# A list-scheduled attention kernel: tap copies spread in time, later and shared PSUM banks, and a new order of the schedule

## The chip, the cores and the metric

One core of one Trainium2 chip. The metric is the device time of one execution in microseconds (us), median of several. Nearly all executions of a kernel agree within 0.3%; one execution of the kernel before took 926.79 us, is not a fast run and is left out of every comparison. A profile's span is about 2 us shorter than the device time of the same run.

Engines: PE (matmul), PEld (its weight loads), DVE (VectorE), ACT (ScalarE), POOL (GpSimd), SP (issues the DMAs).

## The reference, cut to what matters

Two attentions over the same `x` (2048 tokens, 640 wide, 32 heads of 20), mixed by a gate:

```python
g = sigmoid((x * gate_w).sum(-1, keepdims=True))
a = A_ref(x, A_wqkv, A_wo)   # full softmax attention, 32 heads, 2048 x 2048 scores each
b = B_ref(x, B_wqkv, B_wo)   # sliding window: 8 keys per query, at distances 0, 2, ..., 14
return g * a + (1 - g) * b
```

Attention A needs 32 x 2048 x 2048 exponentials. The kernel cuts them into 2048 *units*: one unit is one head, 128 keys and 512 queries, that is 512 columns on 128 partitions.

## The kernel before

The program is written by a small planner inside the kernel. It places every task by an estimated duration, engine by engine. A main loop lays tile after tile of attention A; everything else ("side work": projections, window attention B, folds into the output) is a set of generators that get a turn when PE has a gap.

```python
score = [ps(1536, "score0"), ps(1536, "score1")]      # 3 PSUM banks each
obank = ps(512, "obank")
sbank = ps(512, "side0")
BANKS = [(sbank, 0), (score[0], 1024), (score[1], 1024)]   # banks that side work may take
```

So the PSUM's eight banks are: two scores of three banks each, one output accumulator, one private side bank. The *third* bank of each score is shared. A tile always has two units; if the third bank is free, a third unit goes into it, and this *third position* is used in one of two ways:

```python
def next_tile():
    free = not bank_used[x] and bank_free[x] <= now + XTOL and not crowded(x)
    n = 3 if free else 2
    while len(us) < n and cur["g"] < NG:
        ...
        if len(us) == 2 and not ride:
            ride = wanted([...])      # DVE makes this exponential by integer shifts (a "ride")
            if ride:
                break
        us.append(g * 64 + lo)        # else ACT takes 1536 columns in one piece
```

If side work holds the third bank, ACT takes 1024 columns. Side work asks for a bank by priority (a lower number goes first). The private bank is open to all; a score's bank is not:

```python
elif req[0] == "bank":
    ...
    if best and not force and (ent[0] > xprio() or any(...)):   # best 1 or 2: a score's bank
        return False

def xprio():     # how low a priority may still take a score's bank
    return XPRIO if bdone[0] >= (sch.avail["pe"] - XT0) / (XT1 - XT0) * BALL else XLATE
```

`XPRIO` is 2.5. `XLATE` (6.6) holds when the window work is behind its pace. The priorities are 5 for folds, 6 for window blocks, 6.5 for their projections, so before the change all three may take a score's bank when window work is late.

Three more pieces of side work: the weights of attention B are spread by POOL (the "tap copies"), in bursts; the window block takes a bank; the fold takes four bank turns.

```python
def gen_bweights():
    for m in (2, 0, 1):
        ...
        for c in range(CN):            # five copies in a row on POOL
            T("pool", 1.6, lambda e, o=o, i=i: e.tensor_copy(o, i), ...)

def gen_fold(qc, hu):                  # waits for window block 2*qc+hu and for A's heads
    for blk in (2 * hu, 2 * hu + 1):
        for hf, (c0, c1) in enumerate(((0, 512), (512, D))):
            b = yield from bank()      # also for the 128 columns left over
            ...
```

`gen_prefold` does the same for the last quarter of the tokens and needs the last window block (`gen_b(7)`); only then can the last output rows be finished.

## Time and profile before

| | before |
|---|---|
| device time, fast runs | 873.97 to 875.44 us, median of the four runs 875.15 with the slow one |
| span of the profile | 872.9 us |
| PE / ACT / DVE / POOL busy | 98% / 95% / 78% / 25% |
| exponentials on ACT (L1410) | 815.6 us in 785 pieces |
| units by ride on DVE (L1400) | 300 of 2048 |

The profile page of the kernel before, part 1 (busy us, share of the span, instructions):

```profile
PE 852.7 (98%) x13106; PEld 308.0 (35%) x13106; DVE 680.7 (78%) x1157; ACT 831.0 (95%) x819; POOL 221.1 (25%) x324
```

PE's 98% is not what it seems: the kernel fills PE's gaps with matmuls whose result nobody reads (L1476), and they count as busy. The Trainium skill, "Perfetto Trace Analysis", Identifying the Most-Contended Engine, says that a busy PE is not a good measure of its nearness to its limit and that for ACT and DVE the busy share is a fair one. PE's share misleads for a further reason, the kernel's own: 1472 filler matmuls, 114 of the 853 us, are in the busy count. ACT is the engine to look at.

The groups view of the kernel before, shapes kept apart (line, engine, operation, out and in, count, busy us, mean ns, idle before, what ended it):

```profile
L1410 ACT ACTIVATE ebuf<-score 128x1024 bf16<-128x1024 f32 x607 | 581.6, 1035 | 16.1 <-PE score L1387 12.6 <-ACT ebuf L1410 0.3
L1410 ACT ACTIVATE ebuf<-score 128x1536 bf16<-128x1536 f32 x178 | 251.1, 1476 | 4.7 <-PE score L1387 4.5
L1400 DVE TENSOR_SCALAR uD<-score 128x512 int16<-128x512 f32 x300 | 201.9, 684 | 59.4 <-PE score L1387 57.2 <-ACT g L671 0.5
L489 PE MATMUL side<-xT,kvw 128*32 128x256 bf16 x1380 | 57.4, 276 | 0.4 <-DVE qkvB L773 0.2
L489 PE MATMUL score<-xT,kvw 128*32 128x256 bf16 x1020 | 41.8, 274 | 0.0
```

The third positions: 178 wide pieces on ACT and 300 rides on DVE, 478 together. The last two lines are B's projections: 1020 of their 2400 matmuls write into a score's bank.

Waits of ACT, and the end of the run (groups in order of time: start, us, what) of the kernel before:

```profile
ACT ebuf L1410 <- PE score L1387: 17.1, 53, 1.6
ACT stage L969 <- PE side L950: 6.7, 1, 6.7
```

```profile
841.89 0.42 DVE L880 SCALAR_TENSOR_TENSOR oB<-side,rB 128x256 bf16<-128x256 f32 x1 [0.28 <-PE side L489]
...
856.74 3.77 ACT L1410 ACTIVATE ebuf<-score 128x1536 bf16<-128x1536 f32 x3 [0.24 <-PE score L1387]
867.19 0.60 ACT L969 ACTIVATE stage<-side 128x512 bf16<-128x512 f32 x1 [6.68 <-PE side L950]
```

The first of these lines is the last task of the last window block: it ends at 842.3 us. The last exponential ends at 860.5 us, the run at 872.9 us: a *tail* of 12.4 us.

### The profile page before, as it was taken

The numbers are of one execution on the slowest core, as the hardware profiler recorded it, in microseconds if no ns is written. First come the engines' busy times: TensorE is split into PE (matmuls) and PEld (weight loads), VectorE is DVE, ScalarE is ACT, GpSimd is POOL, SyncE is SP. The second block draws the span as 40 slices with busy tenths as digits, with TensorE's granted clock in tenths as the row PEclk, the third lists the DMA queues.
The fourth block names the chain that finished last, engine by engine and source line by source line (L and its number), as shares of the span: only waits on it lengthen the run. The fifth ranks groups of instructions, "written<-read, shape, count | busy, mean of one in ns | idle before, by whom it ended". The sixth has DMA issues, their size and how long they took to land.

```text
span 872.9 us, 30620 instructions
## 1 busy us (share of the span) xinstructions
PE 852.7 (98%) x13106; PEld 308.0 (35%) x13106; DVE 680.7 (78%) x1157; ACT 831.0 (95%) x819; POOL 221.1 (25%) x324
## 2 busy tenths in 40 slices
PE   8999999999999999999999999999999999999997
PEld 4333233333333333343333333333333334433233
DVE  6567777698988797779687787798788758889953
ACT  5999999899999999999999999999999999999994
POOL 5032014622332231112232122323104312023310
PEclk9999999999999999999999999999999999999999
DMA  9111212101011010010000110010001000100100
GB/s 296 32 38 42 44 34 51 36 15 30 26 28 24 28 36 16 13 37 21 20 18 14 30 26 19 29 27 16 12 20 34 21 19 30 30 6 9 27 6 32
DMA packets 40891, 28.15 MB, mean 32 GB/s; under 512 B 23732, under 2 KB 39556, under 8 KB 40756
## 3 DMA queue, kind: packets, MB, share of 16 engines
q1 hardware_dynamic: 40756, 26.20, 11.3%
q8 instruction: 104, 1.70, 0.8%
q14 instruction: 31, 0.25, 0.1%
HBM read 11.94 MB, written 2.62 MB: 17 GB/s over the span
## 4 chain that ended last, share of the span: by engine, by line
PE 73%; ACT 17%; DVE 6%; issue 4%; DMA 0%; POOL 0%; SPq 0%; DVEq 0%; ACTq 0%
PE score L1387 23%; PE obank L1455 17%; ACT ebuf L1410 16%; PE side L489 14%; PE score L489 9%; PE obank L1476 3%; PE score L1476 2%; PE side L1476 1%; DVE uD L1400 1%; DVE eD L720 1%; DVE stage L789 1%; DVE qkvB L773 1%; PE side L802 1%; PE score L609 1%; DVE stage L865 0%
## 5 line engine op out<-in xcount | busy, mean ns | idle before, releaser
L1410 ACT ACTIVATE ebuf<-score 128x1024 bf16<-128x1024 f32 (+1 forms) x785 | 815.6, 1135 | 20.8 <-PE score L1387 17.1
L1387 PE MATMUL score<-qT,kT 32*128 32x512 bf16 x2048 | 315.0, 385 | 11.0 <-ACT ebuf L1410 4.9
L1400 DVE TENSOR_SCALAR uD<-score 128x512 int16<-128x512 f32 x300 | 201.9, 684 | 59.4 <-PE score L1387 57.2
L712 POOL TENSOR_SCALAR vS<-vA 128x84 bf16<-128x84 bf16 x225 | 142.8, 638 | 161.4 <-PE obank L1455 151.8
L1387 PEld LDWEIGHTS score<-qT,kT 32*128 32x128 bf16 x2048 | 77.7, 91 | 277.4 <-issue 113.3
L1455 PE MATMUL obank<-ebuf,vA 128*21 128x512 bf16 x1748 | 167.4, 385 | 1.2 <-ACT ebuf L1410 0.9
L720 DVE TENSOR_SCALAR eD<-uD 128x2048 int16<-128x2048 int16 x225 | 154.7, 712 | 7.6 <-PE obank L1455 7.0
L687 POOL TENSOR_TENSOR rcp<-rcp,gA 128x16 f32<-128x16 f32 x31 | 10.5, 337 | 429.1 <-DVE rcp L685 429.1
L1455 PE MATMUL obank<-eD,vS 128*21 128x512 bf16 x900 | 78.3, 379 | 0.0
L1455 PEld LDWEIGHTS obank<-ebuf,vA 128*21 128x21 bf16 x1748 | 41.4, 89 | 85.0 <-issue 70.3
L489 PE MATMUL side<-xT,kvw 128*32 128x256 bf16 (+1 forms) x1540 | 70.5, 287 | 0.4 <-DVE qkvB L773 0.2
L489 PE MATMUL score<-xT,kvw 128*32 128x256 bf16 (+1 forms) x1220 | 60.4, 292 | 0.0
L1476 PE MATMUL obank<-xT,zero 128*32 128x512 bf16 x680 | 55.7, 384 | 0.0
L789 DVE TENSOR_TENSOR stage<-qkvB 128x1280 bf16<-128x1280 bf16 x64 | 53.3, 859 | 0.1
L865 DVE TENSOR_TENSOR stage<-qkvB,repB 128x1280 bf16<-128x1280 bf16 x64 | 53.2, 856 | 0.1
L489 PEld LDWEIGHTS side<-xT,kvw 128*32 128x32 bf16 x1540 | 36.9, 96 | 24.4 <-issue 15.0
L489 PE MATMUL side<-stage,ident 128*32 128x512 bf16 (+1 forms) x672 | 44.9, 352 | 0.0
L1476 PE MATMUL score<-xT,ident 128*32 128x512 bf16 x424 | 36.7, 381 | 0.0
L489 PEld LDWEIGHTS score<-xT,kvw 128*32 128x32 bf16 x1220 | 28.6, 96 | 22.3 <-issue 15.2
L692 POOL TENSOR_TENSOR oN<-oTt,rcp 128x512 bf16<-128x512 f32 x31 | 34.9, 1124 | 2.4
L681 DVE STREAM_TRANSPOSE oTt<-obank 128x512 f32<-128x512 f32 x32 | 22.8, 712 | 15.3 <-PE obank L1455 15.0
L1455 PE MATMUL obank<-uD,vA 128*21 128x512 bf16 x300 | 29.2, 379 | 0.0
(174 smaller groups left out, 686.6 us busy)
## 6 DMA issues: line engine op xcount, KB each, us to landing
repB<-eB SPq DMA_DIRECT2D x128, 32.0 KB
WqP<-in_A_wqkv_dram SPq DMA_DIRECT2D x16, 160.0 KB
stage<-in_B_wqkv_dram SPq DMA_DIRECT2D x1, 2400.0 KB
oTd<-oN SPq DMA_DIRECT2D x108, 20.0 KB
qT<-dst SPq DMA_DIRECT2D x104, 20.0 KB
out_dram<-outsb SPq DMA_DIRECT2D x12, 160.0 KB
kvw<-in_A_wqkv_dram SPq DMA_DIRECT2D x2, 800.0 KB
oTd<-in_A_x_dram SPq DMA_DIRECT2D x2, 640.0 KB
```

Source lines behind the costliest of these rows:

```text
L489: ins = e.matmul(o[j:k, :], l[:, j:k], r, start=(first and i == 0), stop=(last and i == n - 1), skip_group_check=True)
L681: T("dve", dvc(512), lambda e: e.transpose(oTt[:, :], obank[:, :]), reads=["obank"], writes=["oTt"])
L692: T(en, c2, lambda e: e.tensor_tensor(oo, ii, ib, ALU.mult), reads=["rcp", "oTt"], writes=["oN0"])
L712: T("pool", 0.7, lambda e, k=k: e.tensor_scalar(vS[:, d % 2, k - 1, :], _ap(vA, (kb * NQ + q) * 4 * DV, [[1, 4 * DV]]), WEIGHTS[k], None, ...
L720: T("dve", 0.11 + 0.1334 * n, lambda e, k=k, sl=sl: e.tensor_scalar(eD[:, sl % NS, 0:512 * n].bitcast(I16), uD[d % 2][:, 0:512 * n].bitcas ...
L789: TB(dvc(CN * TOK, 2), lambda e, w=w, ks=ks: e.tensor_tensor(prodB(w), qB[:, :, :], ks, ALU.mult), reads=["qB", "kB"], writes=[("prod", w) ...
L865: TB(dvc(CN * TOK, 2), lambda e, w=w, vs=vs, rr=rr: e.tensor_tensor(prodB(w), vs, rr, ALU.mult), reads=["vB", ("repB", w4 % 2)], writes=[( ...
L1387: ins = e.matmul(o, kT[32 * j:32 * j + 32, q, kb * P:(kb + 1) * P], qT[g % NQT][32 * j:32 * j + 32, :], start=True, stop=True)
L1400: t = T("dve", 0.69, lambda e: e.tensor_scalar(uD[d % 2][:, 512 * i:512 * (i + 1)].bitcast(I16), side[x], UOFF, 0.0, op0=ALU.add, op1=ALU. ...
L1410: exps[s] = T("act", actc(512 * n), lambda e: e.activation(ebuf[s % NE][:, 0:512 * n], score[s % 2][:, 0:512 * n], ACTF.Exp, scale=LN2 / S ...
L1455: ins = e.matmul(obank[32 * j:32 * j + DV, :], v, src, start=(kb == 0), stop=(last and k >= len(lst) - 4), skip_group_check=True)
L1476: ins = e.matmul(o[32 * j:32 * j + 32, :], w[:, 32 * j:32 * j + 32] if best else w[:, :], xT[:, 0, 0:512], start=bool(best), stop=bool(bes ...
```

## The change

The intent: take the POOL burst apart, hold PSUM banks for a shorter time and fewer turns, and lay the schedule in an order tuned for that. Nothing of the arithmetic changes. The core of the diff:

```diff
 # tap copies: the next one only when POOL is not behind PE
             for c in range(CN):
+                while sch.avail["pool"] > max(sch.avail["pe"], clock[0]):
+                    yield ("cond",)
 # QK sums: the bank is taken when the operand is nearly ready
+                yield ("pe", 0.0, sch.ready(("qabs", (n - 1) % 2)) - 0.2)
                 b = yield from bank()
 # window logits: likewise
+        yield ("pe", 0.0, sch.ready(*[("prod", w) for w in range(WIN)]) - 0.7)
         b = yield from bank()
 # B projections: nine bank turns a block become eight, two of the three leftovers share one
-        for m in range(3):
-            for f0 in range(0, CN, 2):
+        for grp in (((0, 0), (0, 1)), ((0, 2), (0, 3)), ((1, 0), (1, 1)), ((1, 2), (1, 3)), ((0, 4), (1, 4)),
+                    ((2, 0), (2, 1)), ((2, 2), (2, 3)), ((2, 4),)):
 # fold: the two 128-column remainders share one bank, four turns become three
+        b = yield from bank()
+        for k in range(2):
+            yield from mm_group(b, mms(side[b][:, k * P:(k + 1) * P], 2 * hu + k, 512, D), rd, mmc(P), per=3)
 ...                                      (a BATCH table that batches nothing; other cuts)
 # order
-    DVE_AHEAD = 0.4          +    DVE_AHEAD = 0.56
-    BOOST = 4.5              +    BOOST = 4.1
-    XLATE = 6.6              +    XLATE = 6.3
-    XT0 = 150.0              +    XT0 = 144.0
-    QPRIO, KPRIO = 0.9, 2.0  +    QPRIO, KPRIO = 1.1, 1.2     # two lines in the kernel
-    BT1 = 880.0              +    BT1 = 927.0
-    XTOL = 0.2               +    XTOL = 0.17
-    DLOW = 7.0               +    DLOW = 6.7
-    SLACK = (0.3, 0.7)       +    SLACK = (0.3, 0.68)
-    fold priority 5          +    PF = 6.6                    # window 6 and projections 6.5 stay
```

More of the change, by code (lines that the diff above doesn't have):

```diff
@@ L572, in _build @@
     qkeys = {}
+    BATCH = (0, 1, 2, 3, 4)
     def gen_qd():
@@ L578, in gen_qd @@
         for qc in range(QCN):
+            batch = []
             for f in range(CN):
@@ L601, in gen_qd @@
                   reads=[("dst", i)], writes=[("qabs", n % 2)])
+                batch.append(f)
+                n += 1
+                if BATCH[f] != f:
+                    continue
+                fl = [(ff, (n - 1 - f + ff) % 2) for ff in range(max(0, batch[0] - 1), f + 1)]
+                yield ("pe", 0.0, sch.ready(("qabs", (n - 1) % 2)) - 0.2)
                 b = yield from bank()
-                fl = [(f - 1, (n + 1) % 2)] if f else []
-                fl.append((f, n % 2))
-                yield ("pe", mmc(512) * len(fl), sch.ready(("qabs", n % 2)))
+                yield ("pe", mmc(512) * len(fl), sch.ready(("qabs", (n - 1) % 2)))
                 def fn(e, b=b, fl=fl):
@@ L618, in gen_qd @@
                 release(b, t)
+                pc = [p_ for ff in batch for p_ in pieces[ff] if p_[0] >= 4 or qc > 1]
+                gs = sorted({POS[qc, p_[0] // 4] for p_ in pc})
                 hs = [h for h, o, r, m in pc if r + m == DH]
@@ L630, in gen_qd @@
                   dma=True, nd=len(runs))
-                n += 1
                 for q in range(NQ):
-                    if chunks_of(q)[-1] == f and (q or qc > 1):
+                    if chunks_of(q)[-1] in batch and (q or qc > 1):
                         g = POS[qc, q]
                         qkeys[g] = [("qTd", g % NQT, ff) for ff in chunks_of(q)] + [
-                            ("qTb", g % NQT, ff) for ff in sorted({max(ff for ff in range(CN) for p_ in pieces[ff] if p_[0] == h)
+                            ("qTb", g % NQT, ff) for ff in sorted({BATCH[max(ff for ff in range(CN) for p_ in pieces[ff] if p_[0] == h)]
                                                                    for h in range(4 * q, 4 * q + 4)})]
                         done[("q", g)] = True
+                batch = []
     def gen_v(half):
@@ L753, in gen_bproj @@
                 T("dve", 0.1, lambda e, t_=t_: e.memset(t_[:, :, 0:PADB], 0.0), writes=[key, ("kst", 0), ("kst", 1)])
-        for m in range(3):
+        for grp in (((0, 0), (0, 1)), ((0, 2), (0, 3)), ((1, 0), (1, 1)), ((1, 2), (1, 3)), ((0, 4), (1, 4)),
+                    ((2, 0), (2, 1)), ((2, 2), (2, 3)), ((2, 4),)):
+            m, f0 = grp[0]
             while m == 2 and u > 0 and not done.get(("bp", u - 1)):
                 yield ("cond",)
-            if u > 0 and m > 0:
+            if u > 0 and m > 0 and f0 == 0:
@@ L758, in gen_bproj @@
                 bb, key = ((kB, "kB"), (vB, "vB"))[m - 1]
                 TB(0.15, lambda e, bb=bb: e.tensor_copy(bb[:, :, 0:PADB], bb[:, :, TOK:TOK + PADB]), reads=[key], writes=[key])
-            for f0 in range(0, CN, 2):
-                fs = range(f0, min(CN, f0 + 2))
-                b = yield from bank()
-                for f in fs:
-                    mms = [(side[b][:, (f - f0) * TOK:(f - f0 + 1) * TOK],
-                            kvw[:, (m * CN + c) * D + f * P:(m * CN + c) * D + (f + 1) * P],
-                            xT[:, c, t0:t0 + TOK]) for c in range(CN)]
-                    yield from mm_group(b, mms, [("wBp", m)] + XT(t0 // 512), mmc(TOK), first=True, per=2)
-                yield ("dve",)
-                n = len(fs)
-                tt, off, key = dst[m]
-                o = tt[:, f0:f0 + n, off:off + TOK]
-                i = sap(b, 0, [[TOK, n], [1, TOK]])
+            b = yield from bank()
@@ new lines, in gen_bproj @@
+            for k, (mm_, f) in enumerate(grp):
+                mms = [(side[b][:, k * TOK:(k + 1) * TOK],
+                        kvw[:, (mm_ * CN + c) * D + f * P:(mm_ * CN + c) * D + (f + 1) * P],
+                        xT[:, c, t0:t0 + TOK]) for c in range(CN)]
+                yield from mm_group(b, mms, [("wBp", mm_)] + XT(t0 // 512), mmc(TOK), first=True, per=2)
+            yield ("dve",)
+            parts = [(m, f0, len(grp))] if grp[0][0] == grp[-1][0] else [(mm_, f, 1) for mm_, f in grp]
@@ L773, in gen_bproj @@
+            for k, (mm_, f, n) in enumerate(parts):
+                tt, off, key = dst[mm_]
+                o = tt[:, f:f + n, off:off + TOK]
+                i = sap(b, k * TOK, [[TOK, n], [1, TOK]])
                 t = TB(dvc(n * TOK), lambda e, o=o, i=i: e.tensor_copy(o, i), reads=[("side", b)], writes=[key])
-                release(b, t)
-            if m == 1:
+            release(b, t)
+            if grp == ((0, 4), (1, 4)):
                 done[("bqk", u)] = True
@@ L883, in gen_b @@
         done[("b", u)] = True
-    pre = lambda i: (dst2[:, 0:1024], qabs2[:, :], stage[:, 2048:3072])[i].bitcast(FP32)
+    pre = lambda i: (dst2[:, 0:1024], qabs2[:, 0:1024], stage[:, 2048:3072])[i].bitcast(FP32)
     tail_bank = {}
@@ L982, in gen_fold, with mms @@
             yield ("cond",)
-        for blk in (2 * hu, 2 * hu + 1):
-            ob = outsb[blk % 2]
+        rd = [("oTd", qc % 2, q) for q in range(NQ)] + ["woA_d", "woBp"] + [
+            ("oB", hu, f0) for f0 in range(0, CN, 2)]
+        def mms(o, blk, c0, c1):
             tok = slice(blk * P, (blk + 1) * P)
-            rd = [("oTd", qc % 2, q) for q in range(NQ)] + ["woA_d", "woBp"] + [
-                ("oB", hu, f0) for f0 in range(0, CN, 2)]
-            for hf, (c0, c1) in enumerate(((0, 512), (512, D))):
-                b = yield from bank()
-                mms = [(side[b][:, 0:c1 - c0], oB[:, f, tok], woBp[:, f, c0:c1]) for f in range(CN)]
-                mms += [(side[b][:, 0:c1 - c0], oTd[:, qc % 2, f, tok], woA_d[:, f, c0:c1]) for f in range(CN)]
-                yield from mm_group(b, mms, rd, mmc(c1 - c0), per=(1 if hf == 0 else 3))
-                yield ("dve",)
-                t = T("dve", dvc(c1 - c0), lambda e, ob=ob, b=b, c0=c0, c1=c1: e.tensor_copy(ob[:, c0:c1], side[b][:, 0:c1 - c0]),
-                      reads=[("side", b)], writes=[("outsb", blk % 2, hf)])
-                release(b, t)
-            row = qc * 512 + blk * P
-            T("sp", 2.5, lambda e, ob=ob, row=row: e.dma_start(out_v[row:row + P, :], ob[:, :]),
-              reads=[("outsb", blk % 2, 0), ("outsb", blk % 2, 1)], writes=[("out", row)], dma=True)
@@ new lines, in mms @@
+            return [(o, oB[:, f, tok], woBp[:, f, c0:c1]) for f in range(CN)] + [
+                (o, oTd[:, qc % 2, f, tok], woA_d[:, f, c0:c1]) for f in range(CN)]
+        for k in range(2):
+            b = yield from bank()
+            yield from mm_group(b, mms(side[b][:, :], 2 * hu + k, 0, 512), rd, mmc(512))
+            yield ("dve",)
+            t = T("dve", dvc(512), lambda e, b=b, k=k: e.tensor_copy(outsb[k][:, 0:512], side[b][:, :]),
+                  reads=[("side", b)], writes=[("outsb", k, 0)])
+            release(b, t)
@@ new lines, in gen_fold @@
+        b = yield from bank()
+        for k in range(2):
+            yield from mm_group(b, mms(side[b][:, k * P:(k + 1) * P], 2 * hu + k, 512, D), rd, mmc(P), per=3)
+        yield ("dve",)
+        for k in range(2):
+            t = T("dve", dvc(P), lambda e, b=b, k=k: e.tensor_copy(outsb[k][:, 512:D], side[b][:, k * P:(k + 1) * P]),
+                  reads=[("side", b)], writes=[("outsb", k, 1)])
+        release(b, t)
+        for k in range(2):
+            row = qc * 512 + (2 * hu + k) * P
+            T("sp", 2.5, lambda e, k=k, row=row: e.dma_start(out_v[row:row + P, :], outsb[k][:, :]),
+              reads=[("outsb", k, 0), ("outsb", k, 1)], writes=[("out", row)], dma=True)
@@ L1014, in _build @@
     clock = [0.0]
-    DVE_AHEAD = 0.4
+    DVE_AHEAD = 0.56
     DAHEAD = 0.5
@@ L1052, in step @@
         return moved
-    BOOST = 4.5
+    BOOST = 4.1
     XBOOST = 4.0
     XPRIO = 2.5
-    XLATE = 6.6
-    XT0 = 150.0
+    XLATE = 6.3
+    XT0 = 144.0
     XT1 = 860.0
@@ L1164, in v_out @@
             done[("v", kb0 + i, 0)] = True
-    QPRIO = 0.9
-    KPRIO = 2.0
+    QPRIO = 1.1
+    KPRIO = 1.2
     turn(0, 0, 3, 0)
@@ L1252, in _build @@
     BT0 = 230.0
-    BT1 = 880.0
+    BT1 = 927.0
     BALL = 186.0
@@ L1257, in _build @@
     DWAIT = 1.0
-    XTOL = 0.2
+    XTOL = 0.17
     RFILL = 0.0
@@ L1296, in wanted @@
         return None
-    DLOW = 7.0
+    DLOW = 6.7
     DHIGH = 1.0
@@ L1507, in _build @@
     HOLD = 2
-    SLACK = (0.3, 0.7)
+    PB = 6.0
+    PP = 6.5
+    PF = 6.6
+    SLACK = (0.3, 0.68)
     FILL = 0.85
@@ L1587, in _build @@
                     for uu in range(2 * QCN):
-                        add_gen(gen_b(uu), 6 + 0.01 * uu)
-                        add_gen(gen_bproj(uu), 6.5 + 0.01 * uu)
+                        add_gen(gen_b(uu), PB + 0.01 * uu)
+                        add_gen(gen_bproj(uu), PP + 0.01 * uu)
                     add_gen(gen_prefold(), 2.2)
@@ L1593, in _build @@
                     for qq in range(2 * QCN - 2):
-                        add_gen(gen_fold(*divmod(qq, 2)), 5 + 0.01 * qq)
+                        add_gen(gen_fold(*divmod(qq, 2)), PF + 0.01 * qq)
             xheld[0] = None
```

## The prediction

> **What bounds it now.** The page gives PE 98% busy, ACT 95%, DVE 78% of 872.9 us. PE is padded: by windows the filler matmuls (L1476) take 114 of its 853 us. So ACT is the bound, through the exponentials (L1410): 815.6 us (groups view), in 607 pieces of 1024 columns and 178 of 1536, together 1748 units of 512 columns, 0.467 us a unit. Between 50 and 850 us ACT is busy 47.3 to 49.8 us of every 50. The waits give it only 17.1 us before L1410, all on PE's scores. The other 300 of the 2048 units go to DVE (L1400): 0.68 us each plus 225 shifted copies of 0.71 us (L720), about 1.2 us of DVE for a unit that saves ACT 0.467 us. DVE has about 190 us unused, but a ride needs a PSUM bank free of side work and a DVE not behind. The lever is the number of L1400 instructions; the 1536-column form saves next to nothing a unit (0.470 against 0.479 us).
>
> **What the change does.** No arithmetic is removed.
> - B projections: 9 bank turns a block become 8 (8 blocks); fold: 4 become 3 (6 folds). 14 turns fewer at roughly 2 us (PE group, then a 0.68 us copy): estimate 28 us of bank time.
> - QK-sum bank (20 times) and window-logit bank (8 times) taken when the operand is nearly ready: estimate 0.5 us each, 14 us.
> - BATCH holds five different entries, so it batches nothing.
> - BT1 880 to 927 lets DVE's window work lag: 186 us of it over 697 instead of 650 us, about 12 us late in the run, 10 units.
> - Tap copies on POOL (L736): 15 of 1.35 us, now three bursts of five. In the burst at 154.7 us one L720 pass took about 2.7 instead of 0.66 us, and ACT then waited 1.55 us. The Trainium skill, "GPSIMD Engine Reference", Key points, says that POOL shares its SBUF interfaces with VectorE and contends with its 2-port modes; the trace agrees. Spread, 1 to 2 us of ACT idle back, since each copy can still meet a pass.
> - New priorities: sign unknown.
>
> **On the critical path.** If half of the 42 us of bank time is usable at 1.1 us a ride (0.69 DVE, 0.39 PE), and DVE's pace limits it too, I expect 300 to become about 318 rides: ACT loses 18 x 0.467 = 8.4 us. [...] Add 1.5 us from POOL, subtract 2 us of new waits: net 8 us. Start (30 us) and tail after the last exponential (860.5 to 872.9 us) stay.
>
> Predicted 867 us, range 857 to 875. Faster by over 2% (below 857.4): 0.12; within 2%: 0.85; slower: 0.03.
>
> **What would show it.** L1400 count 310 to 330, L1410's sum down 5 to 14 us; ACT's waits for L1387 at or under 17 us; no L720 pass over 2 us, no five L736 in a row; fewer fillers; last exponential near 854 us; tail still about 12 us.
>
> **What would make it wrong.** If rides stay near 300, bank turns were not what held them back: then within 2 us of before. If rides rise but ACT's waits rise too, PE became the bound. If lagging window work piles up before the end, the last folds move into the tail and give the gain back. If rides go well over 340, it is faster by more than 2%.

## The result, and the profile after

Device time after: 862.32 to 862.90 us, median 862.48 us (4 runs). The ratio to the kernel before is 0.986 (95% interval 0.9841 to 0.988): 1.4% faster, inside the 2% band. A ratio here is the mean time of one kernel's fast runs over that of the other's fast runs in the same rounds, so it is not quite the ratio of the medians quoted. Runs of different rounds are compared through their ratios to the kernel before.

Line numbers moved: L1410 became L1432 (exponential), L1400 L1422 (ride), L1387 L1409 (scores), L736 L746 (tap copies), L880 L892 (window block's output), L969 L981 (tail). Page part 1 and groups of the kernel after:

```profile
PE 837.2 (97%) x13299; PEld 310.4 (36%) x13302; DVE 692.4 (80%) x1178; ACT 820.2 (95%) x766; POOL 220.4 (26%) x333
```

```profile
L1432 ACT ACTIVATE ebuf<-score 128x1024 bf16<-128x1024 f32 x458 | 442.4, 1035 | 12.6 <-PE score L1409 9.9 <-ACT ebuf L1432 0.6
L1432 ACT ACTIVATE ebuf<-score 128x1536 bf16<-128x1536 f32 x273 | 382.7, 1470 | 7.2 <-PE score L1409 6.2
L1422 DVE TENSOR_SCALAR uD<-score 128x512 int16<-128x512 f32 x312 | 208.5, 684 | 41.8 <-PE score L1409 39.3 <-ACT g L679 0.4
L489 PE MATMUL side<-xT,kvw 128*32 128x256 bf16 x2400 | 91.4, 274 | 0.9 <-DVE dst L593 0.6 <-DVE qkvB L784 0.2
```

Waits of ACT, and the end of the run, after:

```profile
ACT ebuf L1432 <- PE score L1409: 16.0, 41, 1.0
ACT stage L981 <- PE score L962: 6.3, 1, 6.3
```

```profile
816.65 0.41 DVE L892 SCALAR_TENSOR_TENSOR oB<-side,rB 128x256 bf16<-128x256 f32 x1
...
846.30 2.18 ACT L1432 ACTIVATE ebuf<-score 128x1536 bf16<-128x1536 f32 x2 [0.20 <-PE score L1409]
854.82 1.09 ACT L981 ACTIVATE stage<-score 128x512 bf16<-128x512 f32 x2 [6.34 <-PE score L962]
```

What to read there. The span fell by 12.5 us: ACT is busy 10.8 us less and idle 1.7 us less (span less busy: 41.9 and 40.2 us). There are 12 more rides, but 95 more wide pieces: 585 third positions against 478. All 2400 projection matmuls of B are now in the side bank; the group in the score banks is gone. The last window block ends at 817.1 us, 25 us earlier, and the tail is 11.9 us, as before.

ACT's saving splits like this. Over the 14 profiles, a least-squares fit of the exponentials' busy time gives 0.081 us a piece and 0.429 us a unit. So 53 fewer pieces (785 to 732) are 4.3 us, and 12 units fewer 5.1 us: 9.4 of the 11.1 us that the exponentials fell (815.6 to 804.5). The fit misses single profiles by up to about 2 us, so the split is less sure than the sum (see `narrow` below). The Trainium skill, "ScalarE: Activation LUTs", What ACT_TABLE_LOAD costs, gives 186 ns + 0.833 ns a column for one such instruction, with about 93 ns of overlap between neighbours; for 1024 and 1536 columns that is an estimate of 1039 and 1466 ns, and the trace has 1035 and 1470 ns. The fixed part left after the overlap, 93 ns by the page, is what each piece fewer saves (the fit has 81 ns); two wide pieces replace three narrow ones, so one wide piece saves half of that.

### The profile page after: what moved, and what is told of

Same layout as the page of the kernel before. It is cut to its first block, busy times and chain, and to the rows that moved or that the text cites. A ratio compares the mean times of both kernels' runs of the same rounds, so it can differ in the third digit from the quotient of the medians.

```text
span 860.4 us, 30961 instructions
## 1 busy us (share of the span) xinstructions
PE 837.2 (97%) x13299; PEld 310.4 (36%) x13302; DVE 692.4 (80%) x1178; ACT 820.2 (95%) x766; POOL 220.4 (26%) x333
## 4 chain that ended last, share of the span: by engine, by line
PE 77%; ACT 15%; DVE 4%; issue 3%; POOL 1%; DMA 1%; DVEq 0%; ACTq 0%
PE score L1409 23%; PE side L489 19%; PE obank L1477 18%; ACT ebuf L1432 14%; PE score L489 6%; PE obank L1498 4%; PE score L1498 3%; PE side L1498 1%; PE score L615 1%; PE side L814 1%; DMA oTd<-in_A_x_dram 1%; DVE uD L1422 0%; DVE oTt L689 0%; PE score L1125 0%; ACT xT L1139 0%
## 5 line engine op out<-in xcount | busy, mean ns | idle before, releaser
L1432 ACT ACTIVATE ebuf<-score 128x1024 bf16<-128x1024 f32 (+1 forms) x732 | 804.5, 1197 | 19.9 <-PE score L1409 16.0
L1409 PE MATMUL score<-qT,kT 32*128 32x512 bf16 x2048 | 292.1, 384 | 8.7 <-ACT ebuf L1432 6.3
L1422 DVE TENSOR_SCALAR uD<-score 128x512 int16<-128x512 f32 x312 | 208.5, 684 | 41.8 <-PE score L1409 39.3
L720 POOL TENSOR_SCALAR vS<-vA 128x84 bf16<-128x84 bf16 x234 | 140.7, 604 | 230.7 <-PE obank L1477 186.4
L1409 PEld LDWEIGHTS score<-qT,kT 32*128 32x128 bf16 x2048 | 72.1, 91 | 260.9 <-issue 131.5
L1477 PE MATMUL obank<-ebuf,vA 128*21 128x512 bf16 x1736 | 160.8, 384 | 2.2 <-DVE oTt L689 0.8
L489 PE MATMUL side<-xT,kvw 128*32 128x256 bf16 (+2 forms) x2530 | 102.5, 279 | 0.9 <-DVE dst L593 0.6
L489 PEld LDWEIGHTS side<-xT,kvw 128*32 128x32 bf16 (+1 forms) x2530 | 60.5, 96 | 35.0 <-issue 19.8
L1498 PE MATMUL score<-xT,ident 128*32 128x512 bf16 x628 | 53.0, 381 | 0.1
L784 DVE CAST qkvB<-side 128x512 bf16<-128x512 f32 (+1 forms) x72 | 41.7, 589 | 6.7 <-PE side L489 6.1
L689 DVE STREAM_TRANSPOSE oTt<-obank 128x512 f32<-128x512 f32 x32 | 22.8, 712 | 14.5 <-PE obank L1477 14.3
L1477 PEld LDWEIGHTS obank<-eD,vS 128*21 128x21 bf16 x936 | 23.4, 92 | 17.5 <-issue 2.5
```

The lines of the kernel that those rows point to most:

```text
L489: ins = e.matmul(o[j:k, :], l[:, j:k], r, start=(first and i == 0), stop=(last and i == n - 1), skip_group_check=True)
L720: T("pool", 0.7, lambda e, k=k: e.tensor_scalar(vS[:, d % 2, k - 1, :], _ap(vA, (kb * NQ + q) * 4 * DV, [[1, 4 * DV]]), WEIGHTS[k], None, ...
L784: t = TB(dvc(n * TOK), lambda e, o=o, i=i: e.tensor_copy(o, i), reads=[("side", b)], writes=[key])
L1409: ins = e.matmul(o, kT[32 * j:32 * j + 32, q, kb * P:(kb + 1) * P], qT[g % NQT][32 * j:32 * j + 32, :], start=True, stop=True)
L1422: t = T("dve", 0.69, lambda e: e.tensor_scalar(uD[d % 2][:, 512 * i:512 * (i + 1)].bitcast(I16), side[x], UOFF, 0.0, op0=ALU.add, op1=ALU. ...
L1432: exps[s] = T("act", actc(512 * n), lambda e: e.activation(ebuf[s % NE][:, 0:512 * n], score[s % 2][:, 0:512 * n], ACTF.Exp, scale=LN2 / S ...
```

## The experiments

Two theories were put against each other.

- **Theory A.** The new *order* keeps side work out of the scores' banks; that makes the third positions, and with them ACT's saving. The side work is then pressed into one bank, and the run is only faster if the last window block is done before the last exponential. The code parts matter for that second half.
- **Theory B** (the prediction). Fewer and later bank turns free the banks and make the third positions; the order is a shuffle of unknown sign.

A third suspect was POOL's burst. All twelve kernels gave correct results. The table has every run; the columns are read from the groups, waits and time-ordered views of each profile. "Third" is rides + wide pieces. "Tail" is the span less the end of the last exponential.

| kernel | time, median us | ratio to before | third | exponentials us | ACT waits for scores us | last exponential ends | last window block ends | tail us |
|---|---|---|---|---|---|---|---|---|
| before | 874.0 to 875.2 by round | 1 | 300 + 178 | 815.6 | 17.1 | 860.5 | 842.3 | 12.4 |
| after | 862.5 | 0.986 | 312 + 273 | 804.5 | 16.0 | 848.5 | 817.1 | 11.9 |
| order_only | 875.4 | 1.0013 | 312 + 275 | 804.8 | 21.4 | 854.1 | 858.3 | 18.4 |
| parts_only | 879.5 | 1.0057 | 308 + 165 | 811.8 | 16.6 | 856.7 | 862.6 | 20.2 |
| narrow | 887.9 | 1.0148 | 300 + 0 | 819.5 | 19.4 | 866.1 | 872.2 | 20.3 |
| bar_banks | 893.9 | 1.0216 | 312 + 292 | 802.9 | 25.7 | 855.4 | 878.0 | 36.9 |
| no_spread | 870.3 | 0.9947 | 312 + 278 | 802.0 | 20.1 | 848.8 | 853.8 | 20.0 |
| old_bproj | 872.1 | 0.997 | 312 + 248 | 805.2 | 18.5 | 850.8 | 855.8 | 19.2 |
| old_fold | 873.9 | 0.999 | 312 + 268 | 804.8 | 19.9 | 853.0 | 857.4 | 18.6 |
| held_last | 869.6 | 0.9939 | 312 + 274 | 803.9 | 15.7 | 847.4 | 852.4 | 19.9 |
| old_late | 872.8 | 0.9976 | 304 + 247 | 809.4 | 15.6 | 853.0 | 857.2 | 18.4 |
| xlate_back | 877.1 | 1.0029 | 312 + 224 | 807.1 | 20.3 | 856.1 | 861.0 | 19.2 |
| order_hurry | 870.9 | 0.996 | 312 + 276 | 805.0 | 22.8 | 854.8 | 853.7 | 14.2 |
| retuned | 856.0 | 0.979 | 312 + 285 | 802.3 | 13.8 | 842.6 | 813.6 | 11.4 |

### Order alone and parts alone

`order_only` is the kernel before with all changed constants and none of the code parts. `parts_only` is the kernel after with all constants of before.

```diff
 order_only, against before:   the "# order" lines of the diff above, nothing else
 parts_only, against after:    the "# order" lines taken back, nothing else
```

> The kernel before with only the changed constants (priorities, thresholds, slacks), none of the code parts. A third position is the 512 columns beside the two that a tile always has: a DVE ride or the third part of a 1536-column exponential. Before has 300 + 178 = 478 of them, after 312 + 273 = 585; this build has 312 + 275 = 587. Theory A (the order frees the score banks, and what then decides is whether the last window block ends in time): exponentials busy about 804 us as after, but the schedule that the kernel's own planner lays out puts the last window block 16 us later than before and 38 us later than after, so the tail after the last exponential grows from 12 to about 18 us; time 872 to 878, no gain. Theory B (the prediction: fewer and later bank turns free the banks): without them exponentials stay near 815 us and the time near 875.

> The kernel after with all constants of the kernel before: only the code parts (spread tap copies, late banks, shared banks). This build has 308 + 165 = 473 third positions. Theory A: no gain in ACT (exponentials 811 to 816 us), a longer tail, about 18 us; time 876 to 882, slower than before. Theory B: the 14 saved bank turns and the 28 later ones give most of the gain: 864 to 869.

Measured: order_only 1.0013 (0.999 to 1.0036), so no gain; parts_only 1.0057 (1.0038 to 1.0077), slower. ACT's waits of order_only:

```profile
ACT ebuf L1410 <- PE score L1387: 21.4, 49, 1.6
ACT stage L969 <- PE side L950: 12.8, 1, 12.8
```

The exponentials of order_only, then of parts_only:

```profile
L1410 ACT ACTIVATE ebuf<-score 128x1024 bf16<-128x1024 f32 x455 | 439.9, 1040 | 19.0 <-PE score L1387 16.1 <-PE side L489 0.3
L1410 ACT ACTIVATE ebuf<-score 128x1536 bf16<-128x1536 f32 x275 | 385.9, 1475 | 5.8 <-PE score L1387 5.0
L1400 DVE TENSOR_SCALAR uD<-score 128x512 int16<-128x512 f32 x312 | 208.4, 684 | 45.3 <-PE score L1387 42.7 <-ACT g L671 0.4
```

```profile
L1432 ACT ACTIVATE ebuf<-score 128x1024 bf16<-128x1024 f32 x622 | 596.2, 1039 | 16.8 <-PE score L1409 13.4
L1432 ACT ACTIVATE ebuf<-score 128x1536 bf16<-128x1536 f32 x165 | 235.0, 1478 | 3.9 <-PE score L1409 3.2 <-PE obank L1477 0.2
L1422 DVE TENSOR_SCALAR uD<-score 128x512 int16<-128x512 f32 x308 | 207.0, 685 | 66.5 <-PE score L1409 64.2
```

The order alone gives all of the third positions (587) and all of ACT's saving (exponentials 804.8 us). It loses it again: the last window block ends 4.2 us *after* the last exponential, ACT waits 12.8 us at the end instead of 6.7, and 21.4 instead of 17.1 us along the way. The parts alone give no third position (473 against 478). Theory B falls as stated: the bank turns that the parts save do not become rides. Each half by itself is worth nothing or less; only both together give 12.5 us.

### What a third position on ACT is worth

```diff
-                if ride:
-                    break
+                break          # no third unit for ACT, ever
```

> The kernel after with no 1536-column exponential at all: a third position is used by DVE or not. 300 rides, 874 pieces of 1024 columns. Theory A [...]: 142 more pieces make 12.5 us, 12 fewer rides 5 us: exponentials about 822 us, time 878 to 886. The prediction's reading (a 1536-column piece saves next to nothing a unit): only the 12 rides count, 866 to 869.

Measured: 887.9 us, ratio 1.0148 (1.0131 to 1.0165), which is 2.9% over the kernel after (1.0148 / 0.986) and slightly over what Theory A expected. The exponentials take 15.0 us more than in the kernel after; the fit above gives 11.5 us for 142 more pieces and 5.1 us for 12 units. The other 10 us are mostly the tail (20.3 instead of 11.9 us, which was not expected here: the last window block ends 6.1 us after the last exponential) and 3.4 us of waits for scores. Against the kernel before, which has the same 300 rides, 89 more pieces cost only 3.9 us, 0.044 us a piece and about half of what the fit gives. That a wide piece saves something is shown; its size is known to about a factor of two.

### Keeping side work out of the scores' banks with one constant

`bar_banks` is the kernel before with `XLATE` 6.6 to 4.9: no fold, window or projection task may ever take a score's bank. `xlate_back` is the kernel after with `XLATE` 6.3 to 6.6.

> The kernel before with one constant changed (XLATE 6.6 to 4.9), so that window work and fold may never take a score bank. 312 + 292 = 604 third positions. Theory A: exponentials fall to 800 to 806 us without any of the code parts, but the side work is starved of banks and runs over: tail over 30 us, time 885 to 893. If banks were not what limits the third positions, exponentials would stay at 815 us. If the tail doesn't grow, the time falls to about 862.

> The kernel after with one constant taken back (XLATE 6.3 to 6.6): B projections and fold may take a score bank again when window work is late. 312 + 224 = 536 third positions, 49 fewer than after, so 24 more exponentials: exponentials 2 us longer than after. B projections appear in the score banks again in the groups (none do in after). The planner's last window block is 39 us later: tail 7 us longer, and some new ACT idle: 870 to 876. If that constant is not what keeps the score banks free, it stays at 862 to 864.

Measured: bar_banks 1.0216 (1.0191 to 1.0241), xlate_back 1.0029 (1.0013 to 1.0044). Waits of ACT in bar_banks, then B's projections in xlate_back:

```profile
ACT stage L969 <- PE side L950: 30.9, 1, 30.9
ACT ebuf L1410 <- PE score L1387: 25.7, 58, 1.5
```

```profile
L489 PE MATMUL side<-xT,kvw 128*32 128x256 bf16 x1980 | 77.0, 274 | 0.6 <-DVE qkvB L784 0.5
L489 PE MATMUL score<-xT,kvw 128*32 128x256 bf16 x420 | 17.0, 274 | 0.7 <-ACT ebuf L1432 0.7
```

One number, and no code, lifts the third positions from 478 to 604 and cuts the exponentials by 12.7 us; the last exponential ends 5.1 us earlier. But the starved window work ends 22.6 us after it, and the run is 19 us longer. The way back points the same way: with `XLATE` 6.6 in the kernel after, 420 projection matmuls return to the scores' banks and 49 third positions go. So a bar on side work is enough to make the third positions (bar_banks), and taking `XLATE` back from the kernel after costs 49 of the 107 gained; how the other 58 divide among the remaining constants was not run. And it is a trade: ACT's pieces against the date of the last window block. xlate_back was a little slower than expected.

This has limits. `bar_banks` bars window blocks too, which the change does not; and in `xlate_back` only the first fold (priority 6.60) may come back, the others (6.61 to 6.65) stay barred. Another constant of the order is a rival that no run on the chip tested: `DVE_AHEAD`, which says how far DVE may be booked ahead of PE when side work asks for it. In a count made by building without the chip (medians of 40 builds with `DVE_AHEAD`, `XTOL`, `FILL`, `DLATE` and `DWAIT` nudged by up to 3%), the kernel before has 458 third positions and ends at the planner's 868; with `XLATE` 6.3 and the fold at 6.6 alone it has 546 and ends at 875; with `DVE_AHEAD` 0.56 alone it has 528 and ends at 858. Which constant of the order gives the change its time is therefore not shown.

### The tail by itself

`held_last` is the kernel after with only the last window block held until the planner's 790 us.

```diff
         qc, hu = divmod(u, 2)
+        while u == 7 and sch.avail["pe"] < 790.0:
+            yield ("cond",)
```

> The kernel after with one thing held back: the last window block (half a sequence block) may not start before the planner's 790 us; everything before is unchanged, 312 + 274 third positions, exponentials 804 to 805 us, last exponential near 848.5 us. Theory A: prefold can't start until that block is done, so the tail grows from 12 to about 18.5 us and the time to 868 to 871. Rival: the tail's length has nothing to do with when the last window block ends (PE does the same matmuls there): 862 to 864.

Measured: 869.6 us, ratio 0.9939 (0.9923 to 0.9956), 0.8% over the kernel after. The end of held_last, DVE and ACT in order of time:

```profile
838.64 8.80 ACT L1434 ACTIVATE ebuf<-score 128x1536 bf16<-128x1536 f32 x7
...
851.41 1.00 DVE L894 SCALAR_TENSOR_TENSOR oB<-score,rB 128x512 bf16<-128x512 f32 x2
...
861.71 0.60 ACT L983 ACTIVATE stage<-score 128x512 bf16<-128x512 f32 x1 [14.27 <-PE score L964]
```

The last exponential ends at 847.4 us, 1.0 us earlier than in the kernel after, with the same exponentials within 1 us. Only the end differs: the block ends at 852.4 us and ACT waits 14.3 instead of 6.3 us. No other term of the table differs by more than 1.1 us, so the date of that block is what costs the 7 us.

The table holds the rule: in all eleven builds whose last window block ends within 2 us of the last exponential or after it, the run ends 14.2 to 15.3 us after the block. In the three others (before, after, retuned) it ends 11.4 to 12.4 us after the last exponential. The run ends at the later of the two: last exponential plus 12, last window block plus 14.

`order_hurry` tests it from the other side: order_only with one repair, an early place for the projections of the last window block.

```diff
-                        add_gen(gen_bproj(uu), PP + 0.01 * uu)
+                        add_gen(gen_bproj(uu), (2.45 if uu == 7 else PP) + 0.01 * uu)
```

> The kernel before with the changed constants only (order_only, 872.5 us profiled) and one repair: the B projection of the last window block gets an early place in the order. Third positions as order_only, 312 + 276. Theory A: the last window block ends about 6 us earlier, the tail shrinks from 18.4 to 13 us or less, exponentials unchanged: 867 to 870. If the code parts are needed for the short tail in some other way, 874 to 876.

Measured: 870.9 us, ratio 0.996 (0.9944 to 0.9977). The block ends 4.5 us earlier, the tail falls from 18.4 to 14.2 us, the exponentials stay (805.0 us). The direction and most of the size are as expected; 0.9 us more than the range, because the block still ends only 1.0 us before the last exponential. What order_hurry still lacks to the kernel after is mostly ACT's waiting, 22.8 instead of 16.0 us, and 2.3 us of tail. So a short tail is only part of what the code parts bring; fewer waits for scores are the other part. These waits have no one place: in no 50 us stretch from 50 to 850 us is ACT idle for more than 3.0 us in order_only or order_hurry. Their cause was not followed up.

### Each code part taken back from the kernel after

```diff
 no_spread:  the two "while sch.avail["pool"] > ..." lines removed
 old_bproj:  for m in range(3) / for f0 in range(0, CN, 2) as before
 old_fold:   four bank turns as before
 old_late:   QK-sum and window-logit banks taken at once, as before
```

> The kernel after with the old way of issuing the tap copies on POOL (five in a row). 312 + 278 = 590 third positions, so exponentials busy as after, about 804 us. The kernel's planner sees one 5.7 us hole in ACT near 152 us and a last window block 40 us later than after. Prediction's reading: POOL bursts cost 1 to 2 us of ACT idle through the shared SBUF interface, so 862.5 becomes 864. Theory A with a long tail: 6 us from the tail, and up to 6 us from the hole if DVE's shifted copies really queue behind POOL's copies: 868 to 875.

> The kernel after with the old B projections (nine bank turns a block, no shared bank). 312 + 248 = 560 third positions against 585, so 25 of the 273 wide exponentials are lost: exponentials about 1 to 2 us more; the last window block ends 35 us later than after, so the tail grows by about 6 us. Theory A: 869 to 873. If only bank turns mattered in the sum (8 turns of about 2 us, 1.1 us a ride, half usable: 7 rides, 3 us): 865 to 866.

> The kernel after with the old fold (a bank turn for each 128-column remainder). 312 + 268 = 580 third positions, 5 fewer than after: exponentials the same within 1 us. The last window block ends 37 us later than after, because it waits for the folds. Theory A: only the tail grows, 6 us, with 2 to 4 us of new ACT idle: 869 to 874. If the fold's sharing counts only by its bank time (6 turns, 2 to 3 us): 864 to 866.

> The kernel after with banks for QK sums and window logits taken early again, as before. 304 + 247 = 551 third positions against 585. Theory A: exponentials about 5 us longer than after [...], and the last window block 37 us later, so the tail is 7 to 8 us longer: 872 to 877. Prediction's count (28 turns, 0.5 us each, half usable, 6 rides): 865 to 866.

Measured: ratios 0.9947 (0.9931 to 0.9962), 0.997 (0.9952 to 0.9987), 0.999 (0.9975 to 1.0004) and 0.9976 (0.9957 to 0.9995): 7.6 to 11.4 us slower than the kernel after by the ratios (each over 0.986, times 862.5 us); all four times lie within what Theory A expected. Every one of the four throws the last window block behind the last exponential, and the tail is 6.5 to 8.1 us longer. Only old_late also loses real ACT time (exponentials 809.4 us).

These four numbers must not be added, nor read as the worth of the parts. They sum to over 35 us, and the whole change is worth 12.5 us. The planner is chaotic: a small change anywhere moves the last window block. A count made while building, with no chip time in it, says the same. When five constants of a build are nudged at random 60 times, the planner's own end time has a median of 869 for the kernel before, 872 for parts_only, 861 for order_only and 857 for the kernel after, and from 854 to 860 for the kernel after without one part; the builds as given lie at 858, 865, 860 and 848. In the planner's eyes the order is worth about 9, the parts on top of it about 4, a single part between -3 and 3, and the rest is the choice of a good point. A repeat with other nudges (40, as above) gave 868, 868, 860 and 858, and 858 to 860 without one part, with 458, 457, 568 and 566 third positions. So that parts_only has no more third positions than the kernel before is not the bad luck of one point. What the parts are worth is argued from the planner, not shown on the chip.

### The POOL burst, seen in no_spread

PE, POOL and ACT of no_spread, in order of time, from 149.6 us:

```profile
149.64 7.97 POOL L744 COPY kvw<-stage 128x640 bf16<-128x640 bf16 x5 [7.65 <-PE score L489]
157.59 5.01 POOL L720 TENSOR_SCALAR vS<-vA 128x84 bf16<-128x84 bf16 x9
...
158.09 0.61 PE L1475 MATMUL obank<-ebuf,vA 128*21 128x512 bf16 x4 [4.11 <-POOL vS L720]
159.06 0.61 PE L1407 MATMUL score<-qT,kT 32*128 32x512 bf16 x3
...
159.78 1.02 ACT L1430 ACTIVATE ebuf<-score 128x1024 bf16<-128x1024 f32 x1 [5.42 <-PE score L1407]
```

Five copies stand in POOL's queue before the scaled values (vS) that a ride needs. PE's next task reads vS among other things and waits 4.1 us before its first matmul; the scores stand behind it in PE's queue; ACT starves for 5.42 us. It is in the main a queue behind a queue. The shared port adds little: the last three copies, beside passes of DVE, took 1.66 to 1.70 us, the first two 1.33 and 1.35, so about 1 us in all. In the kernel before the same burst made a smaller hole, by another way:

```profile
154.69 7.97 POOL L736 COPY kvw<-stage 128x640 bf16<-128x640 bf16 x5 [8.05 <-PE score L1387]
155.00 3.35 DVE L720 TENSOR_SCALAR eD<-uD 128x2048 int16<-128x2048 int16 x2
159.59 1.02 ACT L1410 ACTIVATE ebuf<-score 128x1024 bf16<-128x1024 f32 x1 [1.55 <-PE score L1387]
```

Here two of DVE's passes took 3.35 us together while POOL copied (a pass has a median of 0.685 us; the longest of all took 1.83 us), which agrees with the shared SBUF interface that the Trainium skill, "GPSIMD Engine Reference", Key points, describes. After the change the same spot reads:

```profile
152.64 2.75 POOL L746 COPY kvw<-stage 128x640 bf16<-128x640 bf16 x2
155.33 3.21 POOL L720 TENSOR_SCALAR vS<-vA 128x84 bf16<-128x84 bf16 x3
```

Even so, no_spread's last exponential ends only 0.3 us later than that of the kernel after: it makes up for the hole elsewhere (exponentials 802.0 us), and all that it loses in the end is tail.

### A better point

The constants were moved further by a search over the planner's own end time; eleven of them changed.

```diff
-    DVE_AHEAD = 0.56    +    DVE_AHEAD = 0.59
-    XT0 = 144.0         +    XT0 = 142.3
-    DIDLE2 = 0.0        +    DIDLE2 = 0.2
-    DWAIT = 1.0         +    DWAIT = 0.948
-    XTOL = 0.17         +    XTOL = 0.25
-    RFILL = 0.0         +    RFILL = 0.01
-    DLATE = 9.0         +    DLATE = 9.5
-    PP = 6.5            +    PP = 6.56
-    PF = 6.6            +    PF = 6.588
-    SLACK = (0.3, 0.68) +    SLACK = (0.3, 0.676)
-    FILL = 0.85         +    FILL = 0.805
```

> The kernel after with eleven constants moved further (found by a search over the kernel's own planner): 312 + 285 = 597 third positions, 6 fewer exponentials than after, fewer fillers (323 rounds against 408), last window block at the planner's 804 us, as early as after. Theory A: exponentials 0.5 us less, several us less ACT idle, tail as after, 12 us: 854 to 859, faster than both. If the planner's estimates no longer hold on the chip with fewer fillers (lower granted clock, PE late), 860 to 866.

Measured: 855.95 us, ratio to before 0.979 (0.9774 to 0.9806): 2.1% faster than before, though 2% lies inside the interval, and 0.7% faster than the kernel after (0.979 / 0.986). 597 third positions, exponentials 802.3 us, ACT's waits 13.8 us, last window block at 813.6 us, tail 11.4 us. With 1292 filler matmuls instead of 1632 the granted clock was 1.000. It beats both kernels by all three terms at once: pieces, waits, tail.

## Why the prediction was right or wrong

The time (867 us, range 857 to 875; measured 862.5) and the class (within 2%) held. The mechanism held in one half only. That the time came out so near is in part luck: the gain that was to come from bank turns did not come from them, and the order, which the prediction left without a sign, supplied as much.

- **"ACT is the bound", PE padded: right.** ACT's saving of 10.8 us is 86% of the span's 12.5 us.
- **"L1400 count 310 to 330": right, with 312.** "L1410's sum down 5 to 14 us": right, 11.1 us. ACT's waits at or under 17 us: right, 16.0.
- **"The 1536-column form saves next to nothing a unit": wrong.** This term was missing from the sum. The per-unit difference looked small (0.470 against 0.479 us), but the number of wide pieces was free to move: 178 became 273, 53 pieces fewer, 4.3 us by the fit. It about made up for the rides, which came out at 12 more instead of 18 (5.1 us at 0.429 us a unit, instead of 8.4 us at 0.467). A division of busy time by units had put a part of the piece's fixed cost into the unit.
- **"Half of the 42 us of bank time is usable": wrong.** parts_only, which has all of that saving, has 473 third positions against 478. The positions come from the order (order_only: 587), in which B's projections no longer write into the scores' banks. "New priorities: sign unknown" hid the step that mattered most; reading `XLATE` 6.3 against the priorities 6.5 and 6.6 would have shown one part of it.
- **"BT1 880 to 927: 10 units": wrong.** The kernel after with `BT1` put back builds the very same instructions on all five engines, as it does with `BOOST` and `DLOW` put back too. (Built, not run; the built programs are identical.)
- **POOL, "1 to 2 us": the place was right, the mechanism only in part.** The figure "one L720 pass took about 2.7 us" was a misreading: two passes took 3.35 us together. In no_spread the hole was 5.42 us and came mainly through POOL's and PE's queues. "No five L736 in a row" is wrong too: the burst at 59 us still has five; only the later ones are broken up.
- **"Lagging window work piles up before the end and gives the gain back": named among the risks, and this is the whole second half of the story.** It didn't happen in the kernel after (the block ends at 817.1 us) and it happened in every kernel that lacked a part.
- **"Fewer fillers": wrong,** 1632 matmuls against 1472. **"Last exponential near 854 us": too late,** 848.5. **"Tail about 12 us": right,** 11.9.

What stays open: how much each code part is worth once the schedule is tuned for its absence. The single reversals can't say, because each also loses the tuned point. Why old_bproj, old_fold and xlate_back make ACT wait 2 to 4 us more for scores than the kernel after was not followed up (old_late does not, and no_spread has its hole). Open, too, is which constant of the order matters most, `DVE_AHEAD` above all.

## What to carry to other kernels

When side work and the main stream share PSUM banks, count who writes into which bank before costing turns: the number of wide pieces that the shared banks allow can be worth more than any single bank turn, and a single priority threshold can decide it (bar_banks). Look for the second date that ends a run: here the run ends at about the later of the last exponential + 12 us and the last window block + 14 us, so a gain on the first is worth nothing until the second has slack. And with a planner that reacts chaotically, taking one part out of a tuned version measures the loss of the tuning as well; test a mechanism by moving only the task in question (held_last), or by a two-way split of order and parts.

## What the Trainium skill lacked or had wrong

- "GPSIMD Engine Reference", Key points, names the contention of POOL with DVE's 2-port modes but gives no size there (the skill's page on SBUF has slowdowns for other pairs of instructions). Here, in the kernel before, two shifted copies beside a POOL copy burst took 3.35 us together, against a median of 0.685 us for one.
- The larger cost of a POOL burst has no figure in the skill: work queued behind five copies held PE's queue for 4.1 us and ACT for 5.42 us (no_spread). That POOL's queue runs strictly in order the skill does say.
- "Perfetto Trace Analysis", Optimization Strategy, says that consistent bubbles on the saturated engine can mean too little PSUM. Here the lack showed in no bubble: ACT was 95% busy before and after, and the shortage was in the form of its instructions, 178 wide pieces against 273.
- "ScalarE: Activation LUTs" is confirmed: estimates of 1039 and 1466 ns from its formula, 1035 and 1470 ns in the trace.
